# Score and maximum matmuls of an attention kernel, each split into four of 32 output columns

## The chip, the cores and the metric

The kernel runs on one core of a Trainium2 chip. The metric is the device time of one execution in microseconds (us). Five engines matter in the text: PE (matrix multiplication, with its weight loads shown apart as PEld), DVE (vector), ACT (scalar, activation functions), POOL and SP (here mostly the queue that issues DMAs).

## The reference

Two attention layers over the same 2048 tokens of width 576, each with 32 heads of width 18, mixed by a gate. Layer A has keys and values of its own for each head; layer B has one key and one value block for all heads.

```python
def _A_ref(x, wqkv, wo):
    ...
    scores = jnp.einsum("bhqd,bhkd->bhqk", q, k) * scale
    p = _softmax(scores, axis=-1)
    o = jnp.einsum("bhqk,bhkd->bhqd", p, v)
    return (lambda x, *d: x.transpose(*d))(o, 0, 2, 1, 3).reshape(B, S, D) @ wo
def _B_ref(x, wq, wk, wv, wo):
    q = (lambda x, *d: x.transpose(*d))((x @ wq).reshape(B, S, H, Dh), 0, 2, 1, 3)
    k = x @ wk
    v = x @ wv
    ...   # the same with one k and one v
g = _sigmoid((x * gate_w).sum(-1, keepdims=True))
return g * _A_ref(...) + (1 - g) * _B_ref(...)
```

## The kernel before

The 64 heads are taken one after another, the 32 of layer B first, then the 32 of layer A. Until about 330 us the kernel projects x to queries, keys and values and stores them; this part is not touched.

The attention is a loop over steps. A step is one head and one block of 128 keys (for the scores) or of 128 queries (for the maxima); there are 16 steps in a head and 1,024 in all, and the loop takes two steps at once, a step pair. The softmax of a head needs the maximum of each query's row before its exponentials. So each step does two kinds of products of queries and keys. Maxima (`step_max`, L409) run 22 steps ahead: 128 queries are the stationary operand, 512 keys the moving one, the result is a tile `pm` of 128 x 512, and DVE reduces it to one maximum a row (L418). For every second step, one block is done by ACT (Relu of the difference of two key blocks, L412) and DVE (L415) together, which saves one of DVE's passes. Scores (`step_scores`, L446): 128 keys are stationary, 512 queries moving; the result is a tile `ps`, of which ACT takes the exponential into `pt` (L453). The 18 features are held as float16 in a high and a low part, which gives 54 rows of products, and two more rows subtract the maximum, 56 in all.

The data lie twice in the tiles `qs`, `ksa`, `ksb`: from partition 0 for the scores (`SB`), from partition 64 for the maxima (`MB`), so that the two kinds use different row halves of PE.

Four score tiles give the probabilities of 128 keys and 2048 queries. `step_pv` (L459) multiplies them with the values: four float32 matmuls with 19 stationary columns each (18 features and a column of ones for the sum), at columns 0, 32, 64 and 96, all into the one bank `acc`. These use all 128 rows. At a head's end DVE copies `acc` out (L469).

The eight PSUM banks are shared out as three for `ps`, four for `pm` (also used by the output projection, L575) and one for `acc`. PE executes in the order in which the kernel writes; the strings `PLAIN`, `UNIT`, `END`, `AFTER` give that order for a step pair by hand: `s` a score matmul, `m` a maximum matmul, `p`, `P`, `f`, `h`, `H`, `Q` PV groups of 256 or 512 columns, `x` the block shared with ACT, `U` one unit of output projection.

```python
PLAIN = "sA0 mA2 sA1 mA0 sA2 mA3 P sA3 mB0 sB0 mB1 sB1 mB2 h sB2 mB3 sB3 x H"
```

So a score and a maximum matmul stand next to each other, in runs of two or three such couples, and between the runs stands a PV group.

Of the kernel before, what the change touches and what calls it, by code (L numbers as in the profile page):

```python
# [49 lines left out]
def gated_mix_kernel(ctx: ExitStack, tc: tile.TileContext, xT, wall, wv, wo, out):  # L50
    nc = tc.nc
    P = 128
# [27 lines left out]
    qs = [fixed.tile([P, S], F16, name=f"qs{i}") for i in range(3)]  # L80
# [5 lines left out]
    acc = ps_o.tile([P, 512], F32, name="acc")  # L86

    nc.vector.memset(acc, 0.0)
    nc.vector.memset(vb, 1.0)
    nc.vector.memset(ones, MROW)  # L90
    dma(ones_r.rearrange("a (b c) -> (a b) c", c=32), ones)
# [294 lines left out]
    def kst(u):  # L386
        return ksb if u < H else L["ks"][(u - H) % 3]
# [9 lines left out]
    def step_max(u, i, c, low=False):  # L397

        if u not in MX:
            MX[u] = mxs[u] if u < 2 else mxs[2 + u % 3]
        b = SB if low else MB
        if c == "x":
            k = L["kd", u if u >= H else 0][b:b + 54, :]
        else:
            k = kst(u)[b:b + 54, c * 512:(c + 1) * 512]
        pm = ps_m.tile([P, 512], F32, name="pm")
        nc.tensor.matmul(pm, qs[u % 3][b:b + 54, i * P:(i + 1) * P], k, start=True, stop=True)  # L409
        if c == "x":  # L410
            MX["x", u, i] = lead.tile([P, 512], F32, name="xb", bufs=2)
            nc.scalar.activation(MX["x", u, i], pm, AF.Relu)  # L412
        elif c == 0 and ("x", u, i) in MX:
            junk = lead.tile([P, 512], BF16, name="junk", bufs=1)
            nc.vector.tensor_tensor_reduce(junk, pm, MX.pop(("x", u, i)), 1.0, -3e38, op0=OP.add, op1=OP.max,  # L415
                                           accum_out=MX[u][:, i, c:c + 1])
        else:
            nc.vector.tensor_reduce(MX[u][:, i, c:c + 1], pm, axis=AX.X, op=OP.max)  # L418
# [21 lines left out]
    def step_scores(u, i, c, alone):  # L440

        b = SB
        ps = (ps_m if alone and c < 2 else ps_s).tile([P, 512], F32, name="pm" if alone and c < 2 else "ps")
        if alone and c % 2:
            b = MB
        nc.tensor.matmul(ps, kst(u)[b:b + 56, i * P:(i + 1) * P],  # L446
                         qs[u % 3][b:b + 56, c * 512:(c + 1) * 512], start=True, stop=True)
        PT["q"] = PT.get("q", []) + [(c, ps)]
        if alone and c == 0:
            return  # L450
        for c, ps in PT.pop("q"):
            pt = L["pt"].tile([P, 512], F32, name="pt")
            nc.scalar.activation(pt, ps, AF.Exp, scale=SCALE / LIFT ** 2)  # L453
            PT[u, i, c] = pt
# [240 lines left out]
    for T in range(-LEAD, NSTEP + 2, 2):  # L695
# [11 lines left out]
        for op in order.split():  # L707
            k, second, c = op[0], op[1:2] == "B", op[2:]
            if k == "V":
                while len(vunits) > 32 * (-T - 1 - (c == "B")) // LEAD:  # L710
                    project_v(*vunits[0], WV[vunits[0][1]])
                    vunits.pop(0)
            elif k == "x":
                if M + 2 < NSTEP:
                    step_max(*divmod(M + 2, 16), "x")
            elif k in "mM":
                step_max(*divmod(M + second, 16), int(c), k == "M")
            elif k == "s":
                if T < NSTEP:
                    step_scores(*divmod(T + second, 16), int(c), alone)  # L720
            elif k == "U":
                pull(min(units, 1))
                units -= min(units, 1)
            elif T >= 2:
                step_pv(*divmod(T - (2 if k in "pfP" else 1), 16), 256 * (k in "fH"), 256 if k in "ph" else 512)
                if k in "HQ" and T % 16 == 0 and T < NSTEP:
                    head_out(T // 16 - 1)
# [48 lines left out]
```

## Time and profile before

| what | value |
|---|---|
| median of two runs | 2738.94 us (2736.34 to 2741.53) |
| the profiled execution | 2735.79 us, span of its instructions 2734.0 us |
| granted PE clock, mean | 0.991 of full speed |
| busy share of the span | PE 97%, DVE 89%, ACT 87%, POOL 8% |
| instructions of PE | 22,160 matmuls and as many weight loads |
| instruction blocks fetched for PE (queue q8) | 174, 2.85 MB |

The busy share counts the time in which at least one instruction of the engine is under way. A matmul's record covers its passage through PE, about 0.38 us for 512 columns, while the next one can start about 0.22 us later; so a PE that is 97% busy is not PE at its limit, and the distances between starts tell more than the durations. In the chain of waits, the profile follows the work that ended last back to the start and gives each piece to the engine that was then waited for.

### The profile page before, as it was taken

The numbers are of one execution on the slowest core, as the hardware profiler recorded it, in microseconds if no ns is written. First come the engines' busy times: TensorE is split into PE (matmuls) and PEld (weight loads), VectorE is DVE, ScalarE is ACT, GpSimd is POOL, SyncE is SP. The second block draws the span as 40 slices with busy tenths as digits, with TensorE's granted clock in tenths as the row PEclk, the third lists the DMA queues.
The fourth block names the chain that finished last, engine by engine and source line by source line (L and its number), as shares of the span: only waits on it lengthen the run. The fifth ranks groups of instructions, "written<-read, shape, count | busy, mean of one in ns | idle before, by whom it ended". The sixth has DMA issues, their size and how long they took to land.

```text
span 2734.0 us, 57725 instructions
## 1 busy us (share of the span) xinstructions
PE 2663.3 (97%) x22160; PEld 958.8 (35%) x22160; DVE 2430.7 (89%) x4582; ACT 2384.1 (87%) x4768; POOL 231.0 (8%) x438
## 2 busy tenths in 40 slices
PE   5899999999999999999999999999999999999999
PEld 3688522222222222222222333333333332223444
DVE  5345899999999999999999999999999999998875
ACT  3232499999999999999999999999999999998875
POOL 2221000001000200110110001000100020001000
PEclk9899999999999999999999999999999999999998
DMA  7232100001100100110132112112221122122312
GB/s 197 76 118 90 51 20 20 20 18 53 35 17 23 54 27 20 45 43 20 30 66 85 40 51 84 54 40 57 72 66 47 44 61 64 39 64 88 89 36 94
DMA packets 135321, 151.49 MB, mean 55 GB/s; under 512 B 55709, under 2 KB 104765, under 8 KB 133846
## 3 DMA queue, kind: packets, MB, share of 16 engines
q1 hardware_dynamic: 116156, 123.59, 16.2%
q10 hardware_dynamic: 14120, 13.65, 1.5%
q0 software_dynamic: 4768, 10.56, 1.2%
q8 instruction: 174, 2.85, 0.5%
q14 instruction: 103, 0.84, 0.1%
HBM read 92.02 MB, written 46.45 MB: 51 GB/s over the span
## 4 chain that ended last, share of the span: by engine, by line
ACT 54%; PE 37%; DVE 6%; DMA 2%; SPq 1%; issue 1%; DVEq 0%; ACTq 0%
ACT pt L453 48%; PE acc L459 12%; PE ps L446 11%; ACT xb L412 6%; PE ps L210 6%; PE pm L575 4%; DVE mx L418 3%; PE ps L252 2%; PE pm L409 2%; SPq L56 1%; DVE oe L469 1%; DVE junk L415 1%; DMA xs<-xT 0%; DVE oacc L629 0%; DVE oacc L583 0%
## 5 line engine op out<-in xcount | busy, mean ns | idle before, releaser
L453 ACT ACTIVATE pt<-ps 128x512 f32<-128x512 f32 x4052 | 2093.1, 637 | 68.4 <-PE pm L409 60.2
L418 DVE TENSOR_REDUCE mx<-pm 128x1 f32<-128x512 f32 x3096 | 1940.2, 682 | 89.5 <-PE pm L409 74.6
L446 PE MATMUL ps<-qs,ksb 56*128 56x512 f16 x2688 | 818.4, 380 | 10.8
L409 PE MATMUL pm<-ksb,qs 54*128 54x512 f16 x2364 | 738.5, 383 | 2.6 <-DVE mx L418 1.6
L459 PE MATMUL acc<-pt,vb 128*19 128x512 f32 (+1 forms) x6136 | 592.3, 458 | 1.9
L459 PE MATMUL acc<-pt,vg 128*19 128x256 f32 (+1 forms) x5664 | 579.5, 481 | 2.3 <-DVE oe L469 0.5
L409 PEld LDWEIGHTS <-qs 54*128 54x128 f16 x4096 | 330.0, 93 | 248.1 <-issue 195.2
L446 PE MATMUL ps<-qs,ksa 56*128 56x512 f16 x1364 | 404.4, 379 | 4.8 <-ACT pt L453 1.3
L446 PEld LDWEIGHTS <-ksb 56*128 56x128 f16 x2688 | 175.0, 94 | 622.5 <-issue 573.9
L409 PE MATMUL pm<-ksa,qs 54*128 54x512 f16 x1232 | 384.8, 382 | 0.6 <-ACT xb L412 0.4
L415 DVE CUSTOM_DVE_ANT_0 junk<-pm,xb 128x512 bf16<-128x512 f32 x500 | 339.9, 680 | 0.0
L412 ACT ACTIVATE xb<-pm 128x512 f32<-128x512 f32 x500 | 316.5, 633 | 0.0
L446 PEld LDWEIGHTS <-ksa 56*128 56x128 f16 x1408 | 89.3, 94 | 328.9 <-issue 299.0
L459 PEld LDWEIGHTS acc<-pt,vb 128*19 128x19 f32 x6136 | 104.1, 96 | 223.7 <-issue 206.6
L459 PEld LDWEIGHTS acc<-pt,vg 128*19 128x19 f32 x5664 | 96.0, 97 | 222.9 <-issue 204.9
L428 POOL TENSOR_SCALAR mt<-mt 128x32 f32<-128x32 f32 x64 | 18.6, 290 | 1616.4 <-DVE mt L426 1616.4
L214 ACT ACTIVATE ph<-ps,tv 128x512 f16<-128x512 f32 x56 | 38.5, 687 | 122.0 <-PE ps L210 114.5
L409 PE MATMUL pm<-kdb,qs 54*128 54x512 f16 x372 | 141.5, 380 | 0.0
L220 DVE SCALAR_TENSOR_TENSOR pl<-ps,tv,ph 128x512 f16<-128x512 f32 x56 | 42.0, 751 | 93.8 <-ACT ph L214 75.4
L210 PE MATMUL ps<-xh,wh 128*128 128x512 f32 x280 | 76.4, 403 | 3.3 <-DVE xh L277 2.6
L210 PE MATMUL ps<-xh,wl 128*128 128x512 f32 x280 | 75.1, 399 | 0.0
L469 DVE COPY oe<-acc 128x512 f32<-128x512 f32 x63 | 43.6, 692 | 30.0 <-PE acc L459 29.4
(123 smaller groups left out, 1253.8 us busy)
## 6 DMA issues: line engine op xcount, KB each, us to landing
qs<-qkh SPq DMA_DIRECT2D x244, 72.0 KB
qs<-qkl SPq DMA_DIRECT2D x122, 72.0 KB
onh<-oh SPq DMA_DIRECT2D x32, 256.0 KB
onl<-ol SPq DMA_DIRECT2D x32, 256.0 KB
oih<-onh SPq DMA_DIRECT2D x16, 512.0 KB
oil<-onl SPq DMA_DIRECT2D x16, 512.0 KB
ot<-oe SPq DMA_DIRECT2D x220, 36.0 KB
R<-r_d SPq DMA_DIRECT2D x55, 144.0 KB
```

Of the source, the lines that this page charges most:

```text
L210: nc.tensor.matmul(fp, w[a][:kr, k, :], X[b][:kr, k, cs], start=(n == 0), stop=(n == len(PROJ) - 1))
L220: nc.vector.scalar_tensor_tensor(l, fp, t, h, op0=OP.mult, op1=OP.subtract)
L252: nc.tensor.matmul(fp[:, 0:288], X[b][:kr, k, st_ * P:(st_ + 1) * P], w[a][:kr, k, :], start=(n == 0), stop=(n == len(PROJ) - 1))
L409: nc.tensor.matmul(pm, qs[u % 3][b:b + 54, i * P:(i + 1) * P], k, start=True, stop=True)
L412: nc.scalar.activation(MX["x", u, i], pm, AF.Relu)
L415: nc.vector.tensor_tensor_reduce(junk, pm, MX.pop(("x", u, i)), 1.0, -3e38, op0=OP.add, op1=OP.max, accum_out=MX[u][:, i, c:c + 1])
L418: nc.vector.tensor_reduce(MX[u][:, i, c:c + 1], pm, axis=AX.X, op=OP.max)
L446: nc.tensor.matmul(ps, kst(u)[b:b + 56, i * P:(i + 1) * P], qs[u % 3][b:b + 56, c * 512:(c + 1) * 512], start=True, stop=True)
L453: nc.scalar.activation(pt, ps, AF.Exp, scale=SCALE / LIFT ** 2)
L459: nc.tensor.matmul(acc[32 * j:32 * j + 19, a:b], v_of(u, i), PT[u, i, j][:, a:b], start=(i == 0 and a == 0), stop=(i == 15), skip_group_ch ...
L469: nc.vector.tensor_copy(oe, acc)
L575: nc.tensor.matmul(fp[:, 0:288], o[b][:r, t, s2 * P:(s2 + 1) * P], w[a][:r, t, 288 * hf:288 * hf + 288], start=(n == 0), stop=(n == 3 * nt ...
```

## The change

Each score matmul and each maximum matmul becomes four, through a new helper `quarters`: the stationary operand is cut into four pieces of 32 columns, each with a weight load of its own, and each writes 32 partitions of the same PSUM tile. The moving operand is the same for all four. Rows, banks, data types and the order of everything else stay. Lines behind the helper move down by four or five.

```diff
     nc.vector.memset(acc, 0.0)
+
+    def quarters(o, w, x):
+
+        for j in range(0, P, 32):
+            nc.tensor.matmul(o[j:j + 32, :], w[:, j:j + 32], x, start=True, stop=True, skip_group_check=True)
...
         pm = ps_m.tile([P, 512], F32, name="pm")
-        nc.tensor.matmul(pm, qs[u % 3][b:b + 54, i * P:(i + 1) * P], k, start=True, stop=True)
+        quarters(pm, qs[u % 3][b:b + 54, i * P:(i + 1) * P], k)
...
-        nc.tensor.matmul(ps, kst(u)[b:b + 56, i * P:(i + 1) * P],
-                         qs[u % 3][b:b + 56, c * 512:(c + 1) * 512], start=True, stop=True)
+        quarters(ps, kst(u)[b:b + 56, i * P:(i + 1) * P], qs[u % 3][b:b + 56, c * 512:(c + 1) * 512])
```

In the program, PE's tile for a score or maximum matmul was 64 rows by 128 columns and is now 64 rows by 32 columns; PV's tile is 128 rows by 32 columns before and after, and the output projection's is 128 by 128. The wait for a free bank stands on the first quarter, the signal that the tile is complete on the last quarter.

## The prediction

> **What bounds the kernel now.** I read the page first, then the chain of waits stretch by stretch, then the groups by form, then single matmuls in the timeline. The page:
>
> ```profile
> span 2734.0 us, 57725 instructions
> PE 2663.3 (97%) x22160; PEld 958.8 (35%) x22160; DVE 2430.7 (89%) x4582; ACT 2384.1 (87%) x4768; POOL 231.0 (8%) x438
> ...
> q8 instruction: 174, 2.85, 0.5%
> ...
> ACT 54%; PE 37%; DVE 6%; DMA 2%; SPq 1%; issue 1%; DVEq 0%; ACTq 0%
> ACT pt L453 48%; PE acc L459 12%; PE ps L446 11%; ACT xb L412 6%; PE ps L210 6%; PE pm L575 4%; DVE mx L418 3%; PE ps L252 2%; PE pm L409 2%; SPq L56 1%; DVE oe L469 1%; DVE junk L415 1%; DMA xs<-xT 0%; DVE oacc L629 0%; DVE oacc L583 0%
> ```
>
> No engine is the bound alone. The chain is ACT for a little over half of the span and PE for 37%. How they alternate is seen in the chain of 1000 to 1040 us, in the half whose heads share one key block, with the sums by line of that half ahead of it and of the late stretch behind it:
>
> ```profile
> by line: ACT pt L453 57.5%; PE acc L459 12.9%; PE ps L446 12.5%; ACT xb L412 7.5%; DVE mx L418 6.0%; PE pm L409 1.4%; DVE junk L415 1.1%; issue 0.8%; DVE oe L469 0.2%; DVE sm L497 0.1%; DVE m L424 0.1%; DVE mt L426 0.0%; DVE mx L415 0.0%; D
> ```
> ```profile
> 1007.79 0.37 PE ps L446
> ...
> 1013.46 2.54 ACT pt L453 x5
> ...
> 1016.49 3.92 ACT pt L453 x8
> 1020.41 0.49 ACT xb L412
> ```
> ```profile
> by line: PE acc L459 30.4%; PE ps L446 29.9%; PE pm L575 29.2%; ACT pt L453 3.4%; DMA oih<-onh 2.3%; DVE oe L469 1.7%; SPq L56 1.7%; ACT xb L412 0.6%; PE pm L409 0.4%; issue 0.4%
> ```
>
> The first sum is of 330 to 1480 us, the last of 2480 to 2640 us. Around 1010 us, PE sets the pace from 1007.79 to 1013.46 (5.67 us) without waiting; then ACT sets it with its step pair of eight exponentials and one Relu in 3.92 + 0.49 = 4.41 us. From 2480 us on, where output-projection units (L575) are mixed in, the chain is PE almost throughout. So what the change does to PE lands where PE is on the chain, and elsewhere first meets PE's waits.
>
> **What a group costs on PE now.** One step pair issues eight score and eight maximum matmuls (L446 on rows 0 to 63, L409 on rows 64 to 127) and twelve PV matmuls (L459), each of the latter recorded twice:
>
> ```profile
> 1502.23 0.39 PE L446 MATMUL ps<-qs,ksa 56*128 56x512 f16 x1
> 1502.24 0.39 PE L409 MATMUL pm<-ksb,qs 54*128 54x512 f16 x1
> 1502.46 0.38 PE L446 MATMUL ps<-qs,ksa 56*128 56x512 f16 x1
> 1502.46 0.38 PE L409 MATMUL pm<-ksb,qs 54*128 54x512 f16 x1
> 1502.82 0.37 PE L446 MATMUL ps<-qs,ksa 56*128 56x512 f16 x1
> 1502.85 0.37 PE L409 MATMUL pm<-ksb,qs 54*128 54x512 f16 x1
> 1503.15 1.05 PE L459 MATMUL acc<-pt,vg 128*19 128x512 f32 x8
> ...
> 1605.96 0.41 PE L459 MATMUL acc<-pt,vg 128*19 128x256 f32 x4
> 1605.95 0.14 PEld L459 LDWEIGHTS acc<-pt,vg 128*19 128x19 f32 x8 [0.24 <-issue]
> ```
>
> Three things are to be seen. A score matmul and a maximum matmul already run at the same time, on the two row halves, and such a couple follows the one before by 0.23 us where nothing is awaited (1502.23 to 1502.46) and by 0.36 where PE waits. Next, PV's four column tiles already run side by side: the row at 1605.96 is a window that ends as the fourth has started; four matmuls of 0.39 each span 0.41, so they start 0.02 / 3 = 0.007 us apart, and eight loads of about 0.10 span 0.14. Last, a couple, a PV group and an output-projection unit don't overlap: from the last matmul of a couple to PV are 0.30 us (1502.85 to 1503.15), against 0.21 to 0.23 within a run. The chain shows the same on the way back:
>
> ```profile
> 2503.49 0.32 PE ps L446
> 2503.81 0.21 PE ps L446
> 2504.03 0.21 PE ps L446
> 2504.24 1.78 PE pm L575 x12
> 2506.03 0.32 PE ps L446
> 2506.35 0.21 PE ps L446
> 2506.57 0.98 PE acc L459 x8
> ```
>
> The first couple after a PV group, and after an L575 unit, has 0.32 on the chain; the next has 0.21. A switch of shape costs about 0.1 us each way.
>
> **The change part by part.** (1) Nothing leaves: the same 512 moving columns run over the same rows, into the same banks, in the same order; ACT's and DVE's instructions are the same. (2) 8,192 score and maximum matmuls become 32,768, with as many loads. A step pair goes from 16 + 16 + 48 = 80 PE instructions to 64 + 64 + 48 = 176. (3) The wait for the bank stands on the first quarter and the signal on the last one, so nothing new is waited for.
>
> Price of the spread. The eight quarters of a couple (four of scores, then four of maxima) start 0.007 apart if they behave as PV's four do, so the last starts 7 x 0.0068 = 0.048 us after the first; now the second of a couple starts 0.003 behind (0.00 to 0.01 in the rows above). Within a run of couples this costs nothing: each quarter's tile is free 0.213 to 0.23 after its own start, and the next quarter comes for it just then; eight starts need only 0.055. At the end of a run it isn't hidden: PV or L575 waits for the last quarter, which is 0.044 us later. So 0.044 per switch out of a run. How many switches lie on the chain? PV groups have 12% of it, 0.12 x 2734 = 328 us. By the groups by form,
>
> ```profile
> L459 PE MATMUL acc<-pt,vg 128*19 128x512 f32 x2528 | 333.2, 599 | 2.0 <-DVE oe L469 0.5
> L459 PE MATMUL acc<-pt,vb 128*19 128x256 f32 x4080 | 320.4, 386 | 1.9
> L459 PE MATMUL acc<-pt,vb 128*19 128x512 f32 x2056 | 271.9, 601 | 0.0
> L459 PE MATMUL acc<-pt,vg 128*19 128x256 f32 x3136 | 246.2, 386 | 0.4
> ```
>
> there are (4080 + 3136) / 8 = 902 PV groups of 256 columns (0.56 us each on the chain) and (2528 + 2056) / 8 = 573 of 512 (0.98 us), 0.72 on the mean: 328 / 0.72 = 455 on the chain. L575 has 4%, 109 us at 1.78: 61. Together 516 x 0.044 = 23 us. The hand-overs from PE to ACT come 3 x 0.007 = 0.02 later for the last quarter of a score tile; about one in each 18 us of chain, 130 in all: 2.5 us. Lower end: 25 us. Upper end: all 1,475 PV groups and about 65 groups of units pay, 1,540 x 0.044 = 68 us. I take 30, near the lower end, because off the chain PE waits: 1502.46 to 1502.82 alone has 0.13 of it, and a step pair's three switches need 3 x 0.044 = 0.13.
>
> The price of a switch itself. Would it go, now that scores and PV both have 32-column tiles? Tiles go from 64 rows by 128 columns to 64 by 32; PV has 128 by 32, L575 128 by 128. Couple to L575 differs in rows alone (64 against 128) and pays 0.32 - 0.21 = 0.11 all the same, and that is what would be left between quarters and PV. So I keep 0.1 a switch, with 0 as the bound below.
>
> Loads of 32 columns are not in the trace. Bounds: PV's 19-column loads, which start within 0.04 of one another, so nothing; and loads one behind another at about 0.09, so 3 x 0.09 = 0.27 per switch. I take the first, the nearest in columns and in side-by-side tiles.
>
> Issue of instructions: 176 in 4.41 us is one every 0.025 us. What is seen is mixed:
>
> ```profile
> 1605.62 0.09 PEld L409 LDWEIGHTS <-qs 54*128 54x128 f16 x1 [0.28 <-issue]
> 1605.65 0.37 PE L409 MATMUL pm<-kdb,qs 54*128 54x512 f16 x1
> L409 PEldq EVENT_SEMAPHORE  x2: 51/51/51, 1605.5 to 1605.8; - x2
> ```
>
> Behind a wait of the sequencer, a matmul starts 0.03 after its load, as if each instruction took 0.031. But by the program's order 20 instructions lie between these two waits (a load and a matmul, PV's 16 records, a load and a matmul), and the waits start 0.3, at most 0.4 us apart: at most 0.02 each. So I cost issue at nothing: it fits under the streaming. [...]
>
> Instruction fetch: q8's 174 blocks for 44,320 instructions become about 367; at 0.5% of the DMA engines now, that is 1%, hidden.
>
> The sum: span 2734.0 + 30, and 1.8 us around it (the profiled execution took 2735.8): 2766 us. The median shown is 2738.9, so +1.0%.
>
> **The rivals.** A, PE becomes the bound everywhere: the spread is paid at every switch, 2735.8 + 68 = 2804 us. It decides once the waits of PE in ACT's stretches are under 0.13 us a step pair. For it: from 2480 us on that is so already, and maxima end 0.044 later for DVE, which is 3% of the chain. Against: a wait such as 1502.46 to 1502.82 stands in nearly every step pair before. [...]
>
> B, PE's sequencer becomes the bound: 0.031 x 176 = 5.46 us for each of 501 full step pairs, 2735 us, 54 for L575's 864 matmuls and their loads, 330 ahead and some 75 for the last eleven pairs and the end: 3195 us. For it: the row with 0.03. Against: the two waits at most 0.4 apart.
>
> C, faster: the switch between quarters and PV goes, because columns now agree. Then 455 switches lose 0.1 each way, 91 us, and add 23: 2735.8 - 91 + 23 = 2668 us. ACT allows it: 512 step pairs x 4.41 = 2258 and 330 ahead are 2588. Against: couple to L575, where columns agree already, pays in full.
>
> D, the change doesn't do what it says, the quarters run one after another: 3 x 0.213 more for each of eight couples, 5.1 us a step pair, some 5300 us. PV's rows are against it.
>
> **How the numbers follow.** My forecast 0.57, A 0.25, B 0.08, C 0.08, D 0.02. The predicted time is the forecast's, 2766 us. About 2% is what a measurement tells from no change: 2684 and 2794 around the median. The forecast (2745 to 2800) gives 0.53 to the same and 0.04 to slower; A (2780 to 2860) 0.06 to the same and 0.19 to slower; B and D 0.10 to slower; C 0.08 to faster. So faster 0.08, same 0.59, slower 0.33. The range 2715 to 2860 leaves out C, B and D, 0.18.
>
> **What would show it.** Right: quarters of one couple start within 0.05 to 0.06 us; couples in a run still follow at 0.21 to 0.23; the last quarter to PV still 0.30; PE's records of L446 and L409 four times as many; ACT's and DVE's mean durations unchanged; PE's share of the chain a little over 37%. Wrong: a load and a matmul every 0.06 us throughout (B); PV starting in a couple's shadow, under 0.28 after its last quarter (C); couples 0.3 or more apart (loads in line, or D).

## The result, and the profile after

The changed kernel takes 2772.47 us (median; 2772.22 to 2772.71) against 2738.94: a ratio of 1.0122, 95% interval 1.0079 to 1.0166. The profiled execution took 2772.22 us, the span of its instructions is 2770.4. The page of the kernel after, in the lines that answer to those of before:

```profile
span 2770.4 us, 111403 instructions
PE 2708.7 (98%) x46736; PEld 1031.6 (37%) x46736; DVE 2445.7 (88%) x4582; ACT 2413.8 (87%) x4768; POOL 230.6 (8%) x438
...
q8 instruction: 366, 6.00, 0.9%
...
PE 93%; DVE 2%; DMA 2%; ACT 2%; SPq 1%; issue 1%; DVEq 0%; ACTq 0%
```

PE has 24,576 matmuls more and is busy 45 us longer; ACT and DVE have as many instructions as before. On the chain ACT has all but gone (54% before) and PE has 93%. That looks as if PE had become the bound, but the experiments below do not bear it out.

The groups of the page, with the busy time, the mean of one instruction (ns) and the idle time ahead of the group; first three groups before, then those after:

```profile
L453 ACT ACTIVATE pt<-ps 128x512 f32<-128x512 f32 x4052 | 2093.1, 637 | 68.4 <-PE pm L409 60.2
L418 DVE TENSOR_REDUCE mx<-pm 128x1 f32<-128x512 f32 x3096 | 1940.2, 682 | 89.5 <-PE pm L409 74.6
L446 PE MATMUL ps<-qs,ksb 56*128 56x512 f16 x2688 | 818.4, 380 | 10.8
```
```profile
L457 ACT ACTIVATE pt<-ps 128x512 f32<-128x512 f32 x4052 | 2110.8, 616 | 73.3 <-PE pm L93 62.7
L423 DVE TENSOR_REDUCE mx<-pm 128x1 f32<-128x512 f32 x3096 | 1954.8, 683 | 107.8 <-PE pm L93 96.8
L93 PE MATMUL ps<-qs,ksb 56*32 56x512 f16 x10752 | 854.7, 382 | 5.5 <-issue 0.9
L93 PEld LDWEIGHTS <-qs 54*32 54x32 f16 x16384 | 372.7, 89 | 26.3 <-issue 21.4
```

The quarters are in the records: 10,752 score matmuls on `ksb` instead of 2,688, each still 0.38 us. The idle time ahead of the exponentials grew from 68.4 to 73.3 us, that ahead of DVE's reductions from 89.5 to 107.8.

Single matmuls, the timeline of PE at about the time that the prediction showed for the kernel before (not at the same step, because the kernel after is behind by then):

```profile
1502.02 0.40 PE L93 MATMUL ps<-qs,ksa 56*32 56x512 f16 x4
1502.03 0.40 PE L93 MATMUL pm<-ksa,qs 54*32 54x512 f16 x4
1502.24 0.39 PE L93 MATMUL ps<-qs,ksa 56*32 56x512 f16 x4
1502.26 0.39 PE L93 MATMUL pm<-kdb,qs 54*32 54x512 f16 x4
1502.57 0.63 PE L463 MATMUL acc<-pt,vg 128*19 128x256 f32 x8
1503.13 0.40 PE L93 MATMUL ps<-qs,ksa 56*32 56x512 f16 x4
```

Four quarters span 0.40 where one whole matmul took 0.39; a couple is two such rows, and it follows the one before by 0.22 (1502.02 to 1502.24), as before. From the first quarter of the run's last couple to PV are 0.33 us, and from PV of 256 columns to the next couple 0.56. Medians over all such places of the trace give these more finely: couple to couple 0.227 before and after; couple to PV 0.322 before, 0.339 after; PV's second half to couple 0.332 before, 0.329 after. Within a couple, the eight quarters start within 0.023 us.

So PE lost 0.015 us net at each of some 1,500 switches, 22 us in all if nothing absorbed them. The time grew by 33.5. What else changed is seen at the hand-over from PE to ACT. Two exponentials before which ACT had stood idle, in the timelines of PE and ACT; first the kernel before:

```profile
1000.83 0.39 PE L446 MATMUL ps<-qs,ksb 56*128 56x512 f16 x1
...
1001.25 0.60 ACT L453 ACTIVATE pt<-ps 128x512 f32<-128x512 f32 x1
```

and then the kernel after, with a row of its line 457 in the records of ACT's sequencer (count, duration in ns, first and last start):

```profile
1001.05 0.40 PE L93 MATMUL ps<-qs,ksb 56*32 56x512 f16 x4
...
L457 ACTq EVENT_SEMAPHORE  x1: 17/17/17, 1001.5 to 1001.5; - x1
...
1001.55 0.60 ACT L457 ACTIVATE pt<-ps 128x512 f32<-128x512 f32 x1
```

Before, the exponential starts 0.42 us after the score matmul; after, 0.50 behind the quarters, and between the two stands an instruction that was not there, a separate wait in ACT's sequencer. From 480 to 1400 us this is no single case (the rows of the exponentials' line in ACT's records, before and after):

```profile
L453 ACT ACTIVATE pt<-ps x1639: 591/638/767, 479.7 to 1399.7; 128x512 f32<-128x512 f32 x183
```
```profile
L457 ACT ACTIVATE pt<-ps x1619: 591/603/697, 479.8 to 1399.6; 128x512 f32<-128x512 f32 x180
L457 ACTq EVENT_SEMAPHORE  x1617: 17/17/17, 480.0 to 1398.8; - x180
```

Practically each exponential has one, and before there was none. Some exponentials of this stretch had to wait for PE: they start over 0.06 us later behind the one ahead than ACT's closest spacing of 0.477. They are 180 before and 301 after, and for them the median from the start of the last piece of the score matmul to the exponential is 0.423 us before and 0.499 after, with quartiles 0.001 apart. For DVE's reductions it is 0.455 and 0.485; the program has 878 separate waits on DVE before and 882 after.

Where it comes from is read in the program and in the records of both traces. In these each of the 4,096 exponentials carries one wait; where there is a second one, it is an instruction of its own ahead of it (61 before, 4,084 after). An exponential writes a `pt` buffer that an earlier exponential wrote, and it needs PE's signal. Before, one matmul both waited for ACT and signalled to ACT (4,026 of the 4,052 score matmuls in the records), so its signal said that ACT's earlier work was done, and the exponential needed PE's signal alone (4,035 of 4,096). Now the first quarter waits and the last one signals; the last one's signal no longer stands for what the first waited for. The exponential waits for ACT's own earlier instruction itself (4,084 of 4,096), and the wait for PE moves into a separate instruction: 206 separate waits on ACT before, 4,728 after. Most of the new ones stand ahead of exponentials, 498 ahead of the Relu.

### The profile page after: what moved, and what is told of

The parts are those of the page before. It is cut to its first block, busy times and chain, and to the rows that moved or that the text cites. A ratio compares the mean times of both kernels' runs of the same rounds, so it can differ in the third digit from the quotient of the medians.

```text
span 2770.4 us, 111403 instructions
## 1 busy us (share of the span) xinstructions
PE 2708.7 (98%) x46736; PEld 1031.6 (37%) x46736; DVE 2445.7 (88%) x4582; ACT 2413.8 (87%) x4768; POOL 230.6 (8%) x438
## 3 DMA queue, kind: packets, MB, share of 16 engines
q0 software_dynamic: 4768, 10.56, 1.2%
## 4 chain that ended last, share of the span: by engine, by line
PE 93%; DVE 2%; DMA 2%; ACT 2%; SPq 1%; issue 1%; DVEq 0%; ACTq 0%
PE ps L93 40%; PE acc L463 37%; PE ps L215 6%; PE pm L579 4%; PE pm L93 3%; PE ps L257 2%; ACT pt L457 2%; SPq L56 1%; DMA xs<-xT 0%; DVE oacc L633 0%; DVE mx L423 0%; DVE oacc L587 0%; DVE wabs L167 0%; DMA wst<-wall 0%; DMA R<-r_d 0%
## 5 line engine op out<-in xcount | busy, mean ns | idle before, releaser
L457 ACT ACTIVATE pt<-ps 128x512 f32<-128x512 f32 x4052 | 2110.8, 616 | 73.3 <-PE pm L93 62.7
L423 DVE TENSOR_REDUCE mx<-pm 128x1 f32<-128x512 f32 x3096 | 1954.8, 683 | 107.8 <-PE pm L93 96.8
L93 PE MATMUL ps<-qs,ksb 56*32 56x512 f16 x10752 | 854.7, 382 | 5.5 <-issue 0.9
L93 PE MATMUL pm<-ksb,qs 54*32 54x512 f16 x9456 | 759.8, 384 | 1.6 <-DVE mx L423 1.5
L93 PEld LDWEIGHTS <-ksb 56*32 56x32 f16 x10752 | 295.5, 89 | 782.4 <-issue 733.5
L93 PE MATMUL ps<-qs,ksa 56*32 56x512 f16 x5456 | 420.1, 382 | 2.6 <-ACT pt L457 1.0
L93 PE MATMUL pm<-ksa,qs 54*32 54x512 f16 x4928 | 394.8, 383 | 0.0
L93 PEld LDWEIGHTS <-qs 54*32 54x32 f16 x16384 | 372.7, 89 | 26.3 <-issue 21.4
L93 PEld LDWEIGHTS <-ksa 56*32 56x32 f16 x5632 | 143.7, 89 | 393.9 <-issue 365.2
L93 PE MATMUL pm<-kdb,qs 54*32 54x512 f16 x1488 | 145.4, 381 | 0.0
```

The lines of the kernel that those rows point to most:

```text
L93: nc.tensor.matmul(o[j:j + 32, :], w[:, j:j + 32], x, start=True, stop=True, skip_group_check=True)
```

## The experiments

All ratios are against runs of the kernel before on the same chip. The expectations call PE TensorE, ACT ScalarE and DVE VectorE.

**What takes the spread away in part.** `halves`: two pieces of 64 columns instead of four of 32.

```diff
-        for j in range(0, P, 32):
-            nc.tensor.matmul(o[j:j + 32, :], w[:, j:j + 32], x, start=True, stop=True, skip_group_check=True)
+        for j in range(0, P, 64):
+            nc.tensor.matmul(o[j:j + 64, :], w[:, j:j + 64], x, start=True, stop=True, skip_group_check=True)
```

> Each score and maximum matmul as two of 64 columns instead of four of 32. Theory 1 (the later start of the last piece, paid at each switch from a run of couples to PV or to a unit): pieces start 0.0035 us apart in the trace of the changed kernel, so the last of four pieces starts 0.0105 after the first instead of 0.003 (whole) or 0.024 (quarters); a third of the loss, +10 to +14 us over the kernel before. Theory 2 (loads of under 128 columns are slower and stand bare behind a switch): the whole loss stays, +30 to +40 us. Theory 3 (number of PE instructions): also a third; the distance from PV to the first piece tells it from theory 1, which leaves that at 0.33 and 0.54 us.

Measured: 2763.51 us, ratio 1.0108 (1.0094 to 1.0122). The pieces of a couple start within 0.010 instead of 0.023 us, but couples follow at 0.240 instead of 0.227, and couple to PV stays at 0.340. The hand-over to ACT is 0.502, as with quarters, and there are as many separate waits, 4,728. So the loss does not go with the number of pieces; cutting once is enough, and theory 1 and theory 3, which asked for a third of it, fall. The time is near theory 2's, but its reason is not in the trace: from PV's second half to the first piece are 0.330 us, against 0.332 before, so no slower load stands bare there.

`tail_whole`: the changed kernel, but the scores of the last 22 steps, which have no maxima beside them, are whole.

```diff
-        quarters(ps, kst(u)[b:b + 56, i * P:(i + 1) * P], qs[u % 3][b:b + 56, c * 512:(c + 1) * 512])
+        if alone:
+            nc.tensor.matmul(ps, kst(u)[b:b + 56, i * P:(i + 1) * P],
+                             qs[u % 3][b:b + 56, c * 512:(c + 1) * 512], start=True, stop=True)
+        else:
+            quarters(ps, kst(u)[b:b + 56, i * P:(i + 1) * P], qs[u % 3][b:b + 56, c * 512:(c + 1) * 512])
```

> The changed kernel, but with whole score matmuls in the last eleven step pairs, where no maxima are left. The time behind the last head's end is 4.1 us longer with quarters. Theory 1 with the end as a separate loss: -4 us against the changed kernel, so +32 us over the kernel before. Rival, that these 4 us are carried over from the delay ahead: no change, +36.

Measured: 2767.32 us, 1.0126 (1.0111 to 1.0142). The 4 us of the end can't be decided by this: the interval of the changed kernel's ratio covers more than 20 us. In the traces, what follows the last head's copy of `acc` takes 61.6 us before, 65.7 after and 61.8 here, but also 61.4 in `halves`, whose last scores are cut. Most of the loss is made in the loop, as the traces show: from the first head's end to the last one's, the kernel after falls behind by 31 of 36 us, about 0.5 a head. But for the last 22 steps, this run is also a second, closer measurement of the change itself.

**What a given time on PE costs.** `dose48_last` and `dose240_first` leave the matmuls whole and put a redundant piece of a maximum matmul, of 48 or 240 moving columns, ahead of the last or of the first maximum matmul of each run.

```diff
+        if extra:
+            nc.tensor.matmul(pm[:, 0:extra], qs[u % 3][b:b + 54, i * P:(i + 1) * P], k[:, 0:extra],
+                             start=True, stop=True)
...
+            extra = 48 if last and T >= 0 else 0      # dose48_last
+            extra = 240 if since == 1 and T >= 0 else 0      # dose240_first
```

> The kernel before, whole matmuls, but the last maximum matmul of each run of couples (ahead of PV or of a unit) computes its first 48 columns twice, a known piece of PE time at each of some 1540 switches; the trace tells how long (at least 0.020 us by 48 columns at 0.42 ns each). Theory 1 (PE time at a switch is paid in full everywhere): the total grows by the number of switches times the measured piece, +31 us for 0.020. Rival (as predicted: only the third of the switches that lies on the chain pays): a third of it, about +10 us for 0.020.

> The kernel before, but the first maximum matmul of each run computes its first 240 columns twice, at least 0.10 us of PE time in each run, inside it and not at its end. Theory 1 generalised (any PE time in the loop is paid in full, wherever it stands): about 1540 x 0.10 = +154 us or a little more. Rival (PE's waits within the runs take it up, 0.3 us a step pair): under +60 us.

Measured: `dose48_last` 2745.74 us, 1.0045 (1.0033 to 1.0058); `dose240_first` 2762.55 us, 1.0103 (1.0090 to 1.0117). In the trace of the first, a switch from a couple to PV:

```profile
1501.85 0.38 PE L449 MATMUL ps<-qs,ksa 56*128 56x512 f16 x1
1501.85 0.18 PE L410 MATMUL pm<-ksb,qs 54*128 54x48 f16 x1
1501.88 0.37 PE L412 MATMUL pm<-ksb,qs 54*128 54x512 f16 x1
1502.18 0.62 PE L462 MATMUL acc<-pt,vg 128*19 128x512 f32 x4
```

The extra piece starts with the scores, the real maximum 0.03 later, and PV still 0.30 behind that: couple to PV has a median of 0.345 instead of 0.322. The trace has 1,499 extra pieces; by 0.345 - 0.322 = 0.023 they are 34 us of PE's time, and the kernel is 11.7 us slower, a third (9 to 16 us by the interval, a quarter to near a half). ACT's hand-over stays at 0.422. ACT has some 500 separate waits more here, ahead of the Relu; `moving_m` below has as many and is not slower. The larger dose is an estimated 0.11 us (240 of the 512 columns for which couples follow at 0.227; at 0.215, the closest in the trace before, a column is 0.42 ns and the dose 0.10). At some 1,500 runs that is 165 us, of which 28.5 are paid. So theory 1, by which all of it is paid, falls, and in this kernel most of what is added on PE goes into its waits. The changed kernel's 22 us at the switches are worth about 22 / 3 = 7 by this, an estimate; they can't be the 33.

**The separate wait by itself.** `four_q` is the changed kernel with one `pt` tile for the four exponentials of a step, so that only one in four needs a wait for ACT's own earlier work; `four_w` is the kernel before with the same tile.

```diff
-        L["pt"] = ctx.enter_context(tc.tile_pool(name="ppool", bufs=12, side="left"))
+        L["pt"] = ctx.enter_context(tc.tile_pool(name="ppool", bufs=3, side="left"))
...
-            pt = L["pt"].tile([P, 512], F32, name="pt")
+            if (u, i) not in PT:
+                PT[u, i] = L["pt"].tile([P, 4, 512], F32, name="pt")
+            pt = PT[u, i][:, c, :]
```

> The changed kernel with the exponentials of a step written into one tile of four banks' width, three of them, instead of twelve tiles of one; matmuls, banks and order as in the changed kernel. In the program ScalarE then has 1,665 separate waits in its instruction stream instead of 4,728, and one for TensorE ahead of 1,024 exponentials (one of four) instead of all 4,087. Theory W (most of the loss is the separate wait in front of each exponential): exponentials that had waited start again about 0.42 us after the last score piece in three of four cases, and the loss falls from 33 to 10 to 20 us, so 2745 to 2755 us. Rival T (the loss is TensorE's time at the switches, the 15 ns by which they grew): the hand-over plays no part, and the time stays at 2763 to 2773 us.

> The kernel before with the same tile of four banks' width for the exponentials of a step (164 separate waits on ScalarE instead of 206); matmuls whole. It is the control of the run with this tile and quarters. Both theories: within 0.2% of the kernel before, 2733 to 2744 us. If it is 10 us or more faster, the tile itself helps, and what the quarters cost must be counted from here.

Measured: `four_q` 2751.54 us, 1.0065 (1.0051 to 1.0078); `four_w` 2734.83 us, 0.9999 (0.9990 to 1.0008). The records of the line in `four_q`:

```profile
L459 ACT ACTIVATE pt<-ps x1631: 591/625/729, 479.5 to 1399.6; 128x512 f32<-128x512 f32 x182
L459 ACTq EVENT_SEMAPHORE  x408: 17/17/17, 480.6 to 1399.4; - x136
```

One separate wait for each fourth exponential is left. An exponential without one, in the timelines:

```profile
1002.98 0.40 PE L93 MATMUL ps<-qs,ksb 56*32 56x512 f16 x4
...
1003.42 0.60 ACT L459 ACTIVATE pt<-ps 128x512 f32<-128x512 f32 x1
```

0.44 us. Of the 204 exponentials that had to wait in this stretch, 179 have no separate wait, with a median of 0.438 us, and 25, the first of their step, still have it, with 0.498; in the changed kernel it is 0.499. So a separate wait costs 0.06 us at each hand-over that ACT waits for: 0.060 within this one execution, 0.061 between the two kernels. The matmuls, their loads and the switches (0.339 and 0.329) are those of the changed kernel, and half of its loss is gone: 1.0122 (or 1.0126 by `tail_whole`, whose interval lies wholly above this one) less 1.0065 is 0.57%, some 16 us (11 to 22 by the intervals of `tail_whole` and `four_q`). The tile itself does nothing, as `four_w` shows. Theory W holds, and rival T, by which the time would have stayed, falls.

**The same wait without column pieces.** `moving_s` cuts each score matmul along the moving columns, `moving_m` each maximum matmul.

```diff
-        nc.tensor.matmul(ps, kst(u)[b:b + 56, i * P:(i + 1) * P],
-                         qs[u % 3][b:b + 56, c * 512:(c + 1) * 512], start=True, stop=True)
+        for x in range(0, 512, 256):
+            nc.tensor.matmul(ps[:, x:x + 256], kst(u)[b:b + 56, i * P:(i + 1) * P],
+                             qs[u % 3][b:b + 56, c * 512 + x:c * 512 + x + 256], ...)
...   # moving_m instead:
-        nc.tensor.matmul(pm, qs[u % 3][b:b + 54, i * P:(i + 1) * P], k, start=True, stop=True)
+        for x in range(0, 512, 256):
+            nc.tensor.matmul(pm[:, x:x + 256], qs[u % 3][b:b + 54, i * P:(i + 1) * P], k[:, x:x + 256], ...)
```

> The kernel before with each matmul of scores as two pieces of 256 moving columns, one after the other over all 128 output columns: the tile shape, the rows passed and the partner in the array stay, nothing runs side by side that did not before, and the switch out of a run starts from the last piece, so its spread does not grow. As with the quarters, one piece waits for ScalarE and another signals, and ScalarE has 4,229 separate waits instead of 206. Theory W: hand-over to ScalarE about 0.08 us longer, 15 to 30 us slower, 2754 to 2769 us. Rival T: nothing at the switches grew but a second load and start of each score matmul, 0 to 8 us, 2739 to 2747 us.

> The kernel before with each matmul of maxima as two pieces of 256 moving columns. It is the control for cutting a matmul as such: as many more loads and starts as with the scores cut so, but ScalarE has 705 separate waits (206 before) and VectorE 882 (878). Theory W: within 8 us of the kernel before, 2735 to 2747 us. Rival T: the same as for the scores cut in this way, whatever that is, to within 5 us.

Measured: `moving_s` 2749.45 us, 1.0052 (1.0040 to 1.0065); `moving_m` 2735.53 us, 1.0004 (0.9996 to 1.0013). The exponentials' line in the records of the first and of the second, and below them the chain of each by engine:

```profile
L455 ACTq EVENT_SEMAPHORE  x1628: 17/17/17, 480.1 to 1399.8; - x181
L455 ACT ACTIVATE pt<-ps x1628: 591/609/753, 480.3 to 1399.6; 128x512 f32<-128x512 f32 x181
...
PE 91%; ACT 3%; DVE 3%; issue 2%; DMA 1%; SPq 1%; ACTq 0%; DVEq 0%
```
```profile
L455 ACT ACTIVATE pt<-ps x1638: 591/636/766, 479.8 to 1399.8; 128x512 f32<-128x512 f32 x182
...
PE 65%; DVE 16%; ACT 15%; issue 2%; DMA 2%; SPq 1%; POOL 0%; DVEq 0%; ACTq 0%
```

Cutting as such, 4,096 more loads and matmuls, is free where the consumer gains no separate wait (`moving_m`), and costs 14.7 us where each exponential gains one (`moving_s`). In `moving_s` the hand-over from the last piece is 0.366; a piece of 256 columns is recorded 0.380 - 0.271 = 0.109 shorter than a whole one, so without the wait it would be an estimated 0.423 - 0.109 = 0.314, and the wait costs 0.05. Theory W had asked for 15 to 30 us and 0.08: the cause is right, the size at its lower edge. Rival T asked for equal times of the two; they lie 14 us apart.

The chains teach a caution. `moving_s` has PE at 91% of its chain, as the changed kernel has 93%, but `dose240_first`, with 92%, has an estimated 165 us more of PE's time and pays a sixth of it; and `four_q`, too, has 93%. When the piece that signals isn't the piece that waits, the chain goes back along PE's records, and a wait shorter than a matmul's record of 0.38 us is hidden in it; that is how these chains are best explained, and no run tests it.

**What equal tile shapes would be worth.** `scores_only` cuts the scores and leaves the maxima whole.

```diff
-        nc.tensor.matmul(ps, kst(u)[b:b + 56, i * P:(i + 1) * P],
-                         qs[u % 3][b:b + 56, c * 512:(c + 1) * 512], start=True, stop=True)
+        quarters(ps, kst(u)[b:b + 56, i * P:(i + 1) * P], qs[u % 3][b:b + 56, c * 512:(c + 1) * 512])
```

> Quarters for the scores, whole matmuls for the maxima; the two stand next to each other on the two row halves. Shape theory: each couple now holds two tile shapes, so it can no longer run side by side: score quarters and maximum one after the other at 0.3 us each instead of 0.23 for both, eight couples with 0.3 to 0.4 us more each, +2.5 us a step pair, 4000 us or more. Rival (shape matters only where rows of two shapes overlap): about half of the loss of the changed kernel, 2750 to 2765.

Measured, in one run: 6351.88 us, with a granted clock of 0.58 on the mean. Its timeline of PE:

```profile
3000.05 0.62 PE L93 MATMUL ps<-qs,ksb 56*32 56x512 f16 x4
3000.60 0.60 PE L414 MATMUL pm<-ksb,qs 54*128 54x512 f16 x1
3001.13 1.06 PE L463 MATMUL acc<-pt,vb 128*19 128x256 f32 x8
```

The maximum starts 0.55 us behind the scores instead of beside them, and PV 0.53 behind the maximum. Here, tiles of different width on the two row halves don't run together. At this clock single records are longer besides, 0.60 us for a whole maximum against 0.37 to 0.39 before; why the clock fell, no run shows.

The last three ask whether the switch to PV would go if PV had the scores' tile. PV over two row halves is written here with a second bank for its sums, so `pm3` takes a bank from the maxima alone, `pv64_q` also cuts PV in two row halves and uses quarters, and `pv64_w` cuts PV so but leaves scores and maxima whole.

```diff
-    ps_m = ctx.enter_context(tc.tile_pool(name="ps_m", bufs=4, space=PSUM))
+    ps_m = ctx.enter_context(tc.tile_pool(name="ps_m", bufs=3, space=PSUM))      # all three
...
-        for j in range(4):
-            nc.tensor.matmul(acc[32 * j:32 * j + 19, a:b], v_of(u, i), PT[u, i, j][:, a:b], ...)
+        for r, o in ((0, acc), (64, acc2)):      # pv64_q, pv64_w
+            for j in range(4):
+                nc.tensor.matmul(o[32 * j:32 * j + 19, a:b], v_of(u, i)[r:r + 64], PT[u, i, j][r:r + 64, a:b], ...)
```

> The kernel before with three banks for maxima and units instead of four and one left idle: the price of the lost bank by itself, for the two runs with 64-row PV. Expected: DVE and PE wait for each other more, +0 to +80 us; the shape theory makes no statement on it.

> The changed kernel with PV also on tiles of 64 rows by 32 columns: each PV matmul as two of 64 rows, the upper half summed in a second bank (three banks are left for maxima and units instead of four), and one more vector addition at each head's end (0.7 us). All tiles of the loop but the units' then have one shape. Theory 1 with the price of a switch coming from the shape: the 0.1 us at each switch goes, last quarter to PV from 0.32 to under 0.24 us and PV to quarters from 0.33 to about 0.23; PE gains up to 3 x 0.2 us a step pair, ACT's 4.41 us a step pair then sets the pace: 2640 to 2700 us if the missing bank costs nothing. Rival (what is waited for at a switch isn't the shape but the drain of rows or of the moving data): switches stay at 0.32, the lost bank and the extra instructions make it 2780 to 2850.

> The same 64-row PV in two banks, but scores and maxima as whole matmuls of 128 columns (as before). The tiles then differ in columns alone. Shape theory (any difference, rows or columns, costs 0.1 us): switches stay at 0.31 to 0.33 us, and the time is that of a kernel before with three banks, 2740 to 2790. Rival (only a difference in rows costs): as fast as with quarters, or faster by their spread.

Measured: `pm3` 2932.18 us, 1.0722 (1.0704 to 1.0740); `pv64_q` 2855.42 us, 1.0440 (1.0424 to 1.0456); `pv64_w` 2999.84 us, 1.0967 (1.0951 to 1.0983). A run and its PV group in the trace of `pv64_q`:

```profile
1500.44 0.40 PE L95 MATMUL pm<-ksa,qs 54*32 54x512 f16 x4
1500.46 0.40 PE L95 MATMUL ps<-qs,ksb 56*32 56x512 f16 x4
1500.76 0.40 PE L95 MATMUL pm<-ksa,qs 54*32 54x512 f16 x4
1500.77 1.24 PE L466 MATMUL acc<-pt,vb 64*19 64x512 f32 x16
...
1502.23 0.40 PE L95 MATMUL ps<-qs,ksb 56*32 56x512 f16 x4
1502.34 0.40 PE L95 MATMUL pm<-ksa,qs 54*32 54x512 f16 x4
1502.44 0.40 PE L466 MATMUL acc<-pt,vb 64*19 64x256 f32 x4
```

PV starts 0.01 after the maxima (median from the last quarter to PV 0.003, against 0.316 in the changed kernel). That alone would say too much, because PV's first half runs on the rows of the scores, and these began earlier. On the same rows, from the scores to PV are 0.21 us in the second pair of rows, and 0.215 at a quarter of all switches: the distance of two couples. With equal rows and columns the switch is gone. In `pv64_w`, whose PV differs from the couples in columns alone, PV starts 0.303 after the last maximum, and never less than 0.30 after the last score:

```profile
1501.22 0.37 PE L411 MATMUL pm<-ksb,qs 54*128 54x512 f16 x1
1501.52 1.08 PE L462 MATMUL acc<-pt,vb 64*19 64x512 f32 x16
```

So a difference in either is enough to pay. Against `pm3`, equal shapes win 77 us, and PV in halves without them loses 68; but the lost bank costs 197, and none of the three comes near the kernel before. The bank had been expected to cost at most 80 us, and with it the times expected of the other two were missed. No version run here beats the kernel before.

## Why the prediction was right or wrong

**The time.** Forecast 2766, 30 us more than before; measured 2772.5, 33.5 more. Of the +30 that were taken, the composition was wrong: one term was too large, one was missing. The two errors have nearly the same size and opposite signs, so that the sum came out this near is luck.

**The spread, mis-sized.** The last quarter was to start 0.048 after the first; it is 0.023. The spacing had been taken from PV's four, which start 0.007 apart, but each column tile of these has two loads and two matmuls in the records; a quarter has one of each, and its spacing is 0.023 / 7 = 0.0033. That the second load makes the difference fits these rows, but no run takes it apart. At the switch 0.017 to 0.018 came (0.322 to 0.339), and 0.003 went on the way back, so about 0.015 net instead of 0.044.

**How much of it is paid, right.** 516 of about 1,540 switches, 0.34, were counted as on the chain by the shares of its lines. The dose of 0.023 at each switch cost 11.7 of 34 us, 0.34, though its interval leaves a quarter to near a half open. With both, the term is 0.015 x 1,500 / 3, about 7 us instead of 23.

**"Nothing new is waited for", wrong.** This step failed. The waits that the change was seen to add were those on PE; that the split of one instruction into one that waits and one that signals also changes what its consumer has to wait for was not looked at. ACT got 4,522 separate waits, hand-overs that ACT waits for take 0.061 us more by them, and that is some 16 us by `four_q` and 14.7 by `moving_s`. "ACT's and DVE's instructions are the same" holds for their counts and not for the sequencer's. In the traces, the separate wait that was shown begins 0.437 us after the last score piece and lasts 0.017, and the exponential starts 0.045 behind its end, at 0.499; one with the wait in itself starts at 0.438 (`four_q`). What fills the 0.045, no run shows.

**The hand-over term.** 0.02 us at about 130 places was put at 2.5 us. Without the separate wait 0.015 is left at ACT (0.423 to 0.438), so the size was near; DVE has 0.030 (0.455 to 0.485). Of the 33 us, 16 are the separate wait and about 7 the switches; about 10 remain, uncertain by several us. `four_q` kept the separate wait at 98 of its 590 waited hand-overs (330 to 2640 us), so the whole of that term may be an estimated 2 us larger. The rest of the hand-overs is a candidate too (by `moving_s`, 14.7 us for 0.05, ACT's 0.015 would be an estimated 4), and DVE's 0.030. But no run took these away, and so this part stays open.

**Right as told.** A switch keeps its price (last quarter to PV 0.316, before 0.315), and the runs with PV in halves say why rival C could not happen: rows still differ, and one difference is enough. Loads of 32 columns cost nothing: 89 ns each (93 to 94 for 128 columns before), and couples still at 0.227. Issue fits: rival B's 5.46 us a step pair stands against 4.51 measured from 480 to 1400 us (4.42 before). Instruction blocks are 366 (367 predicted), 0.9% of the DMA engines' time, and issue has 1% of the chain as before. Quarters run side by side, eight starts within 0.023 us, so D is out; its 0.213 for a quarter is 0.215 at the closest couples of the trace before. Rival A's full price at every switch is out by the dose, though its sign was right.

**Signs that were told in advance.** The distance of couples, the switch, the number of records and DVE's mean (683 ns, 682 before) came as written. The quarters of a couple were to start within 0.05 to 0.06 us; it is 0.023. PE's share of the chain was to be a little over 37% and is 93%. `four_q` has the same share at half the loss, so the share doesn't tell what costs the time. ACT's mean was to be unchanged and fell from 637 to 616 ns, which is no faster work (see the end).

## What to carry over

Before an instruction is cut in pieces, look at who waits and who signals: if the piece that signals isn't the one that waited, its consumer loses an implied order and may get a separate wait, at 0.06 us a hand-over here. Such a wait stands in no busy time and no count of an engine's instructions (ACT has 4768 before and after); look for it among the sequencer's records of the consumer's line, and at the distance from a producer's start to its consumer's. Price what is added on an engine by a dose in the same place: here a third of it was paid at the switches, whatever the chain's share said.

## What was not expected of the hardware

- Tiles of different width on the two row halves did not run together: 0.55 us from scores to maximum, 6351.88 us in one run, and a granted clock of 0.58 instead of 0.99.
- Tiles that agree in rows and columns need no pause between scores and PV: 0.215 us on the same rows, as between two couples, instead of 0.30. A difference in columns alone costs about as much as one in rows (0.303 and 0.316 from the last maximum).
- An exponential's record gets some 11 ns longer with each one that follows without waiting, though they start 0.477 us apart all the same: from 480 to 1400 us of the changed kernel, from 592 ns to 694 nine places on. Where ACT had to wait, it begins short again. The shorter mean (616 ns, 637 before) thus comes for a good part from ACT's waiting more often, and it is no faster work.
- One PSUM bank fewer for the maxima costs 197 us, 7.2%.
